# A gated linear attention and an MLP on one Trainium2 core: products of zeros at the start, another first product, stores in halves, another written-out order

## Chip, cores and metric

One core of one Trainium2 chip. The metric is the device time in microseconds (us) of one execution of the whole program, lower is better. "TensorE" does the matmuls, "VectorE", "ScalarE" and "GpSimd" the elementwise work, "SyncE" issues nearly all DMAs. In the profile they are PE (with PEld for the loading of weights), DVE, ACT, POOL and SP.

## The reference

A recurrence with a gate for each channel, over 4 batches, 8 heads, 768 positions, 48 channels a head; then, on its output seen as 768 rows of 384, a layer norm, a two-layer MLP with ReLU and a residual.

```python
for t in range(S):                                    # attention; state is 48 x 48 for each batch and head
    state = alpha[:, :, t, :, None] * state + np.einsum('bhd,bhe->bhde', k[:, :, t], v[:, :, t])
    y[:, :, t] = np.einsum('bhd,bhde->bhe', q[:, :, t], state)
x = y.transpose(0, 2, 1, 3).reshape(B, S, H * D)      # (4, 768, 384)
mu, var = mean(x), mean((x - mu) ** 2)                # over the last axis
xn = (x - mu) / np.sqrt(var + 1e-06) * g_ln
out = x + np.maximum(xn @ w_ch1, 0.0) @ w_ch2         # w_ch1 384 x 1536, w_ch2 1536 x 384
```

q, k, v and alpha come in float32. The two weight matrices come in float64 and are rounded to float32 on the chip. All matmuls are in float32.

## The kernel before

**Tiling.** The 768 positions are cut into 6 chunks of 128; a chunk of one batch is one attention block, 24 in all. A block is written as a generator (`attention`, from L220 on) that issues one step at each call: logarithm of the gates (L225, tile `la`), their sums over positions with a triangular matmul (L228, `lps`), two exponentials (L232, L233), k and q multiplied by them (GpSimd L235, VectorE L237), transposes of q and k (L251, `tps`) with copies out of PSUM (L255, L257), scores (L264, `aps`), masked copy (L268, `at`), output (L281 with the state, L286 with the scores, `yps`), copy to `x` (L290), the change of the state (L297, `sps`; L302; L307), statistics and normalisation (L311 to L318, `xn`), transposes of the normalised x (L325, `xps`) and their copy (L327, `xT`).

**Weights.** Twelve pieces of 768 KB are loaded, three in flight (`load_weights`, L151), and rounded by VectorE and ScalarE (`round_weights`, L163 to L178; six pieces of the first matrix, then six of the second). The first chunk's MLP is done plainly: 12 hidden products of 512 columns (`hidden`, L337), then the second layer for each batch in thirds (`project`, L349).

**Chunks 1 to 5** use fewer products. The first layer is done in two halves r = 0 and 1 by 15 products each (`hidden_product`, L510), numbered 0 to 14, in the order of the tuple FIRST. Product n multiplies one combination of blocks of the first weights (`combine_first`, GpSimd L462) with one combination of blocks of xT (`combine_x`, VectorE L486). Product 11 uses a block of xT as it is. Each product's accumulator, one of three in PSUM under the tag "m", is taken off by VectorE or ScalarE, and some of the results are added together later by GpSimd (`add_late`, seven of them in a half: L529, L532, L535, L540, L545, L548, L549). So product 4 is followed by L531 and L532, product 14 by L534 and L535, product 11 by the ScalarE copy L539 and by L540, which adds it to a sum that product 14 began; product 2's accumulator is added by L542 to what L540 wrote, and product 12's by L553 to what L549 wrote. ReLUs (L562) follow on ScalarE. The second layer is done for two batches at a time by seven products of six accumulating matmuls (`product`, L404), in the order 1, 4, 2, 6, 7, 5, 3; the combinations of the hidden values are VectorE's L390. The rows of the second batch of a pair are stored after product 5, those of the first (`o0`) after product 3, each with one DMA of 128 rows of 384 (`send`, L566). The left half of `o0`'s columns has its last addition after product 2 (L417), the right half after product 3 (L430).

**Order.** Every engine runs its instructions in the order in which the program issues them, and waits at each for what it needs. The order is written out by hand in the string ORDER: each letter calls the next step of one generator. Small letters are the attention blocks: a to d are the four batches of chunk 0, e to h those of chunk 1, and so on to x. Capitals A to L are the weight pieces (rounding in three steps, then the issue of the load three pieces on). M is the MLP (each product is two steps: the matmuls, then what takes them off), S the combinations of weights on GpSimd, X those of xT, N those of the hidden values, R the ReLUs. SyncE, too, issues its DMAs in this order and waits at each until its tile is free or written; the loads of q, k, alpha and v of the first chunk and of the first three weight pieces are issued ahead of the string.

**PSUM.** Tag "a" has three buffers for the gates' sums, the transposes and the scores (which take two at once), tag "s" two, tag "m" three for the MLP. A tile takes a buffer whose last reader stands earlier in the order, and waits for it.

The loop that runs the order:

```python
    with tc.manual_schedule():
        for turn in ORDER:
            next(turns[turn], None)
```

Of the kernel before, what the change touches and what calls it, by code (L numbers as in the profile page):

```python
# [9 lines left out]
FP32 = mybir.dt.float32  # L10
# [11 lines left out]


ORDER = (
    "ababdaacbaabccaabacdacbaabadcbbbdcdAabbbdaBcCccdabAeddbcbdcffcdfeegacfcbagdhfbde"
    "adbceBeegAdhfBCfdeabdfefcAheiBeafdeagjgbecfebcfcgeegfdefdgcghhihfdcgdegCCigMhMgD"
    "DhMjEMEjFMhiDkhfMgfighFheMFFfMMIMEIhIDMgEjhMGhMgjMhgfMGiHMMGGkMMMMHeiJMkMlHJMigM"
    "IMLJilHljMejKKjiLKeLjMhhfjSigSMhMlSMglSlhgiffMKkMhMhSSSMSSSMXiXkikXSXiimjMXXXSSM"
    "MXkMMSkjMMXkMkMMSMMjMmMMjXkmMSlmiMSMMiMkMMXkMjMMMlMlmRMmMMMokSjlMlMnlMnMljnkMMMR"
    "MjnMMMMSMMmMnMMmnRMMRRMoRSkiMlpklniMkpnjmMMRMmMRpkMRMNMMNmMlMiRkmMMiNMMnloMpRMSM"  # L30
    "njNMMkplMoRMMMkMMNmjNMMlMMNNmonnMljomqMMlqMMlnXMMXMXmXnXXMXqMMMXmmXMMooMMMMpMpMn"
    "MMXMMoMoMMMrMoXMnRqoRmoMpMMrpMMMMMMpMMpRnproMMmMMmqMMMrMMMqqMsMMnMnMpJqrRnqsMorM"
    "tMMMMmqMooRppMpotsRMMtRMtMrMRqMRNMoMNMRNMMrMpRMoNsMqMspqpMoMtMMRMMMNMNMMNMMMoMpn"
    "MpNsrrnMtrpqvrquXrXXrXMquXqXsMXsrMXrMqMMXMXuMMMMrMrMLMsMtXMMstMMMtqMsstMMMMMqvRR"
    "MMvMsuMsMtuMMRMMMrMMuwMMMMRMMMvwMvqMttqMMMruRMMRMMsMMRMMMMRMssRtwtsvutxvMRNsvMNN"
    "tMvNsRtRMMMvMtMMuusMMtMMwuuMrMMwwxNxMxvrtNNMMMNMMMtxsMMMuXMXXXMvMvuuXxXXMXvXuMMM"
    "MwwXwMMxMMxMXMMMMMMuvMMxMMuMMwRxMMMwwRMvMwMMMRxuxwxwwMuxMRxvMwMMMxxMMMMMRMMvMMuM"
    "RMMMvMMMxMMRuMRMMRMMNMMMNRMMNMMvMMNMMMwwMMvwMxxRNwRMMNMNNMMMMwxMMvxMXXXXXXMMMMXX"
    "XMMMMMMMMMXMMMMMMMMXMMMMMRRMMMMMMMMMMMMMRMMRMMMMMMMMMMRRMMMRMMRMMMMMMRMNMMMNRNMM"
    "MMNMMMMMMMRMNRMNMMNMMMMNMMMMMMMM"  # L40
)


# [1 line left out]
def kernel(  # L45
# [36 lines left out]
    nc = tc.nc  # L82
# [4 lines left out]
    P = 128  # L87
# [8 lines left out]
    cpool = ctx.enter_context(tc.tile_pool(name="const", bufs=1))  # L96
# [5 lines left out]
    ps = ctx.enter_context(tc.tile_pool(name="ps", bufs=2, space=bass.MemoryType.PSUM))  # L102
# [93 lines left out]
    nc.vector.memset(eps, EPS)  # L196
    least = cpool.tile([P, 1], FP32, name="least")
    nc.vector.memset(least, -8.0 * (896 << 20))


    eqs = [cpool.tile([P, NP, 2, 64], FP32, name=f"eq{b}") for b in range(B)]
# [157 lines left out]
    HJ, HM = NJ // 2, DM // 2  # L359
# [13 lines left out]
    def quarters(c, b):  # L373
        if (c, b) not in win:
            hT = hT_of[c]
            a11, a12, a21, a22 = (hT[:, js, i] for i in (b, b + 1)
                                  for js in (slice(0, HJ), slice(HJ, NJ)))
            win[c, b] = {1: a11, 2: a12, 4: a22}, a21
        return win[c, b]
# [14 lines left out]
    def product(c, b, n):  # L394

        if n == 1:
            for i in (0, 1):
                win["o", i] = work.tile([P, 2, HM], FP32, name="ob", tag="ob", bufs=3)
            u = [work.tile([P, 512], FP32, name="u", tag=f"u{i}", bufs=1) for i in range(2)]
            for i in range(4):  # L400
                win["u", i] = u[i // 2][:, i % 2 * HM:][:, :HM]
        acc = ps.tile([P, HM], FP32, name="ops", tag="m", bufs=3)
        for j in range(HJ):
            nc.tensor.matmul(acc, quarters(c, b)[0][n][:, j], win["b"][n][:, j],  # L404
                             start=(j == 0), stop=(j == HJ - 1))
        yield
        x0, x1 = (x_of[c, i].rearrange("p (s m) -> p s m", s=2) for i in (b, b + 1))
        o0, o1 = win["o", 0], win["o", 1]
        p1, u2, u3, u4 = (win["u", i] for i in range(4))
        add, add_late = nc.vector.tensor_add, nc.gpsimd.tensor_add  # L410
        if n == 1:
            nc.scalar.copy(out=p1, in_=acc)
            add_late(o0[:, 0], p1, x0[:, 0])
        elif n == 4:
            add(o1[:, 0], acc, x1[:, 0])
        elif n == 2:
            add(o0[:, 0], acc, o0[:, 0])  # L417
        elif n == 6:
            add(u2, acc, p1)
        elif n == 7:  # L420
            add(u3, acc, u2)
            add_late(o1[:, 1], u3, x1[:, 1])  # L422
            add_late(o1[:, 0], u3, o1[:, 0])
        elif n == 5:
            add(u4, acc, u2)
            add(o1[:, 1], acc, o1[:, 1])
            add_late(u4, u4, x0[:, 1])
            send(c, b + 1, o1)
        else:
            add(o0[:, 1], acc, u4)  # L430
            send(c, b, o0)
            del x_of[c, b], x_of[c, b + 1]
        yield

# [54 lines left out]
            yield  # L489

    RELUS = ((1, 0), (2, 0), (0, 0), (0, 1), (1, 1), (2, 1))
    FIRST = (3, 7, 5, 10, 9, 1, 4, 14, 11, 6, 13, 2, 8, 0, 12)

    def hidden_product(c, r, n):

        if n == FIRST[0] and r == 0:
            hT_of[c] = work.tile([P, NJ, B, P], FP32, name="hT", tag="hT", bufs=1)
        if n == FIRST[0]:
            for i in range(3):
                first_of["u", i] = work.tile([P, 512], FP32, name="u", tag=f"u{i}", bufs=1  # L500
                                             ).rearrange("p (j t) -> p j t", j=2)
        hT = hT_of[c].rearrange("p j b t -> p j (b t)")
        cs = [hT[:, t * NT + 2 * r:][:, :2, h * HB * P:(h + 1) * HB * P]
              for t in range(3) for h in range(2)]
        acc = ps.tile([P, 2, HB * P], FP32, name="hps", tag="m", bufs=3)
        a, b = first_of["a"][n], first_of["b", c][n]
        for i in range(2):
            j = 2 * r + i
            w = a[0][:, j * P:(j + 1) * P] if j < 3 else a[1]
            nc.tensor.matmul(acc[:, i], w, b, start=True, stop=True)  # L510
        yield
        u0, u1, u2 = (first_of["u", i] for i in range(3))
        c0, c1, c2, c3, c4, c5 = cs
        add, sub = nc.vector.tensor_add, nc.vector.tensor_sub
        add_late, sub_late = nc.gpsimd.tensor_add, nc.gpsimd.tensor_sub

        if n == 3:
            nc.scalar.copy(out=c5, in_=acc)
        elif n == 7:
            add(c4, acc, c5)  # L520
        elif n == 5:
            add(c2, acc, c4)
        elif n == 1:
            add(u0, acc, c2)
        elif n == 10:
            nc.scalar.copy(out=u1, in_=acc)
        elif n == 9:
            sub(u2, u1, acc)  # L528
            add_late(c4, c4, u2)  # L529
        elif n == 4:  # L530
            sub(c2, c2, acc)  # L531
            add_late(c2, c2, u1)  # L532
        elif n == 14:
            add(u2, acc, u2)  # L534
            add_late(c0, u0, u2)  # L535
        elif n == 6:
            add(c4, acc, c4)
        elif n == 11:
            nc.scalar.copy(out=c1, in_=acc)  # L539
            add_late(c0, c0, c1)  # L540
        elif n == 2:
            add(c0, acc, c0)  # L542
        elif n == 13:
            sub(c3, u0, acc)
            add_late(c1, c1, c3)  # L545
        elif n == 8:
            sub(u2, u2, acc)
            add_late(c1, c1, u2)  # L548
            add_late(c5, c5, u2)  # L549
        elif n == 0:  # L550
            sub(c3, c3, acc)
        else:
            sub(c5, c5, acc)  # L553
        yield
# [7 lines left out]
                    nc.scalar.activation(out=x, in_=x, func=AFT.Relu)  # L562
                    yield

    def send(c, b, ob):
        nc.sync.dma_start(out[b, c * P:(c + 1) * P], ob.rearrange("p s m -> p (s m)"))  # L566

    def mlp():
        for c in range(NCB):
            if c == 0:  # L570
                for j in range(NJ):
                    yield from hidden(c, j)
                thirds = [range(i * NJ // 3, (i + 1) * NJ // 3) for i in range(3)]
                for b0 in range(0, B, 2):
                    for js in thirds:
                        for b in range(b0, min(b0 + 2, B)):
                            yield from project(c, b, js)
                continue
            for r in range(NT // 2):
                for n in FIRST:  # L580
                    yield from hidden_product(c, r, n)
            for b in range(0, B, 2):
                for n in (1, 4, 2, 6, 7, 5, 3):
                    yield from product(c, b, n)
# [48 lines left out]
```

## Time and profile before

| | us |
|---|---|
| Timed runs, median (lowest to highest), 3 runs | 475.58 (474.87 to 476.09) |
| Profiled run, time | 473.87 |
| Profiled run, first to last instruction (the span) | 471.8 |
| TensorE's first matmul | 4.25 |
| First hidden product of chunk 0 (L337) | 46.34 |
| First product of the last chunk (L510) | 413.85 |
| First L404 product of the last chunk | 441.02 |
| Last addition (L430) starts | 468.60 |

The profile's lines name an engine, a line of the kernel, what is written and what is read with partitions and elements, a count and durations. In the order of time each row is: start in us, length in us, engine, line, operation, and in brackets how long the engine stood idle before it and what it waited for. The table by stage gives for each stretch its length and the busy us of PE, PEld, VectorE, ScalarE and GpSimd with the number of instructions, then the granted TensorE clock, the share of the DMA engines, and GB/s. A row of the waits reads: who waited for whom, us in total, times, longest.

### The profile page before, as it was taken

What the parts mean: (1) busy time and instruction counts of PE and PEld (TensorE: products, weight loads), DVE (VectorE), ACT (ScalarE), POOL (GpSimd) and SP (SyncE); (2) the same over time, 40 slices, a digit from 0 to 9 for tenths busy, and PEclk for the clock granted to TensorE, in tenths of its full rate; (3) what the DMA queues carried; (4) which work ended last, traced back from release to release, by engine and by line L of the source; (5) the groups of instructions that cost most, each with busy time, mean ns of one, the idle gap of its engine ahead of it and who ended that gap; (6) DMA issues with size and microseconds to landing.
All of it is one profiled execution on the core that took longest, in us unless ns stands there. A gap on an engine that the chain in (4) does not pass through costs nothing.

```text
span 471.8 us, 9234 instructions
## 1 busy us (share of the span) xinstructions
PE 459.0 (97%) x3712; PEld 388.5 (82%) x3712; DVE 327.1 (69%) x571; ACT 152.0 (32%) x325; POOL 203.8 (43%) x203
## 2 busy tenths in 40 slices
PE   5989999999999999999999999999999999999997
PEld 3758654566788899988899998899998899987996
DVE  4899997768456985567768378685656576675742
ACT  5676533421132631114341133351203331123300
POOL 5034010049779873127553116573214281145611
PEclk9999999999999999999999999999999999999999
DMA  8988365203112102030211320120010000000000
GB/s 267 334 234 265 78 192 173 83 23 113 52 36 67 35 18 84 8 114 18 86 35 35 100 71 17 35 85 1 33 36 1 1 1 17 18 33 2 0 35 33
DMA packets 32498, 33.84 MB, mean 72 GB/s; under 512 B 13108, under 2 KB 28596, under 8 KB 32456
## 3 DMA queue, kind: packets, MB, share of 16 engines
q1 hardware_dynamic: 31912, 33.12, 22.8%
q8 instruction: 29, 0.48, 0.4%
q10 hardware_dynamic: 544, 0.13, 0.1%
q14 instruction: 13, 0.11, 0.1%
HBM read 28.49 MB, written 4.76 MB: 70 GB/s over the span
## 4 chain that ended last, share of the span: by engine, by line
PE 90%; DMA 4%; DVE 2%; POOL 2%; ACT 2%; SPq 0%; issue 0%; POOLq 0%; DVEq 0%
PE ops L404 29%; PE hps L510 26%; PE hps L337 7%; PE ops L349 7%; PE aps L264 5%; PE yps L286 4%; PE yps L281 4%; PE tps L251 3%; PE lps L228 2%; PE sps L297 2%; PE xps L325 2%; DMA rk<-in_k_dram 2%; DMA ws<-in_moe_w_ch_dram 1%; DMA ra<-in_alpha_dram 1%; DVE w L163 1%; ACT ws L169 0%
## 5 line engine op out<-in xcount | busy, mean ns | idle before, releaser
L307 POOL TENSOR_TENSOR st<-st,gate 128x384 f32<-128x384 f32 x20 | 20.6, 1034 | 76.7 <-issue 30.6
L510 PE MATMUL hps<-sum,w 128*128 128x256 f32 x200 | 51.7, 381 | 0.0
L404 PE MATMUL ops<-w,hT 128*128 128x192 f32 x240 | 42.5, 327 | 0.0
L404 PE MATMUL ops<-w,sum 128*128 128x192 f32 x240 | 42.4, 326 | 0.0
L404 PE MATMUL ops<-ws,hT 128*128 128x192 f32 x240 | 42.3, 326 | 0.0
L562 ACT ACTIVATE hT<-hT 128x512 f32<-128x512 f32 x60 | 36.6, 632 | 16.5 <-POOL hT L548 6.6
L510 PEld LDWEIGHTS hps<-sum,w 128*128 128x128 f32 x200 | 37.1, 190 | 5.2
L404 PEld LDWEIGHTS ops<-w,hT 128*128 128x128 f32 x240 | 39.3, 190 | 0.7
L404 PEld LDWEIGHTS ops<-w,sum 128*128 128x128 f32 x240 | 39.3, 190 | 0.3
L404 PEld LDWEIGHTS ops<-ws,hT 128*128 128x128 f32 x240 | 39.3, 190 | 0.0
L268 DVE COPY_PREDICATED at<-consts,aps 128x512 f32<-128x512 int32 x48 | 32.2, 724 | 10.2 <-PE aps L264 9.9
L286 PE MATMUL yps<-rv,at 128*64 128x48 f32 x768 | 36.4, 219 | 0.0
L422 POOL TENSOR_TENSOR ob<-u,x 128x192 f32<-128x192 f32 x10 | 6.9, 686 | 67.6 <-issue 42.8
L235 POOL TENSOR_TENSOR qk<-rk,ek 128x384 f32<-128x384 f32 x24 | 26.7, 1113 | 19.5 <-ACT ek L232 19.5
L286 PEld LDWEIGHTS yps<-rv,at 128*64 128x64 f32 x768 | 33.0, 137 | 1.3 <-issue 0.7
L529 POOL TENSOR_TENSOR hT<-hT,u 128x512 f32<-128x512 f32 x10 | 12.8, 1284 | 48.6 <-DVE u L528 48.5
L337 PE MATMUL hps<-xT,w 128*128 128x512 f32 x72 | 32.6, 598 | 0.0
L349 PE MATMUL ops<-w,hT 128*128 128x384 f32 x96 | 32.3, 488 | 0.0
L510 PE MATMUL hps<-xT,w 128*128 128x256 f32 x120 | 31.2, 383 | 0.0
L251 PE MATMUL tps<-consts,qk 128*112 128x128 f32 x192 | 29.2, 281 | 1.5 <-DVE at L268 1.0
L264 PE MATMUL aps<-qkT 48*128 48x128 f32 x384 | 28.6, 285 | 1.5 <-DVE at L268 0.8
L251 PEld LDWEIGHTS tps<-consts,qk 128*112 128x112 f32 x192 | 22.8, 137 | 8.8 <-issue 4.1
(127 smaller groups left out, 956.2 us busy)
## 6 DMA issues: line engine op xcount, KB each, us to landing
ws<-in_moe_w_ch_dram SPq DMA_DIRECT2D x12, 768.0 KB
ra<-in_alpha_dram SPq DMA_DIRECT2D x24, 192.0 KB
rk<-in_k_dram SPq DMA_DIRECT2D x24, 192.0 KB
rq<-in_q_dram SPq DMA_DIRECT2D x24, 192.0 KB
rv<-in_v_dram SPq DMA_DIRECT2D x24, 192.0 KB
out_dram<-ob SPq DMA_DIRECT2D x24, 192.0 KB
row<-eq SPq DMA_DIRECT2D x20, 2.0 KB
gate<-row SPq DMA_DIRECT2D x20, 2.0 KB
```

Of the source, the lines that this page charges most:

```text
L235: nc.gpsimd.tensor_mul(qk[:, 1, :, :D], raws.pop(("k", c, b)), ek)
L251: nc.tensor.transpose(tps[:, p], qks[b][:, i, p].rearrange("p a b -> p (a b)")[:, :R], ident)
L264: nc.tensor.matmul(aps[i][:, p], qkT[rows, 1, p], qkT[rows, 0, p], start=True, stop=True)
L268: nc.vector.copy_predicated(out=at[:, i], data=aps[i], mask=mask.unsqueeze(1).broadcast_to([P, NP, P]))
L281: nc.tensor.matmul(yps[s, p].rearrange("p a b -> p (a b)"), qkT[:, 0, p, s], sts[b][:R, p].rearrange("p a b -> p (a b)"), start=True, stop ...
L286: nc.tensor.matmul(yps[s, p, i], at[:, i, p, s], vt[:, 2 * p + i], start=(c == 0), stop=(c == 0 or i == 1))
L307: nc.gpsimd.tensor_mul(st, st, gate.unsqueeze(2).broadcast_to([P, NP, 2 * D]))
L337: nc.tensor.matmul(hps, w1[:, f, j * P:(j + 1) * P], xT_of[c][:, f], start=(f == 0), stop=(f == NF - 1))
L349: nc.tensor.matmul(ops_of[b], hT_of[c][:, j, b], w2[:, j], start=(j == 0), stop=(j == NJ - 1))
L404: nc.tensor.matmul(acc, quarters(c, b)[0][n][:, j], win["b"][n][:, j], start=(j == 0), stop=(j == HJ - 1))
L510: nc.tensor.matmul(acc[:, i], w, b, start=True, stop=True)
L562: nc.scalar.activation(out=x, in_=x, func=AFT.Relu)
```

## The change

Five edits. A tile of zeros is set by VectorE, and nine matmuls of it by itself are issued first of all on TensorE; their result, in a buffer of tag "a", is read by nobody. FIRST starts with product 11, the others keep their order, so in each half product 11 moves from the ninth place to the first. The late addition L540 moves, in the code, from product 11 to product 14, behind that product's own late addition; the order of the seven late additions on GpSimd stays. The rows of `o0` are stored in two halves of 192 columns, the left one after product 2, the right one after product 3. And ORDER is another string, of the same length and with each letter as often as before; only its first lines are shown.

```diff
 ORDER = (
-    "ababdaacbaabccaabacdacbaabadcbbbdcdAabbbdaBcCccdabAeddbcbdcffcdfeegacfcbagdhfbde"
-    "adbceBeegAdhfBCfdeabdfefcAheiBeafdeagjgbecfebcfcgeegfdefdgcghhihfdcgdegCCigMhMgD"
+    "baacabbaadbcdbabcacababadcbdbadabbadbAaacabdcacccbcdBddceecdeCafefhbdAfbdcfbchbf"
+    "BahffeefcbedeededggCcAgffBbeAgBdiadbeadgfecagfeedcegffheghgcfCidcgdgcgkihDCMihMh"
...
+    zero = cpool.tile([P, P], FP32, name="zero")
+    nc.vector.memset(zero, 0.0)
+    idle = ps.tile([P, 512], FP32, name="lps", tag="a", bufs=3)
+    for _ in range(9):
+        nc.tensor.matmul(idle[:, :P], zero, zero, start=True, stop=True)
...
             add(o0[:, 0], acc, o0[:, 0])
+            send(c, b, o0, (0,))
...
-            send(c, b, o0)
+            send(c, b, o0, (1,))
...
-    FIRST = (3, 7, 5, 10, 9, 1, 4, 14, 11, 6, 13, 2, 8, 0, 12)
+    FIRST = (11, 3, 7, 5, 10, 9, 1, 4, 14, 6, 13, 2, 8, 0, 12)
...
             add_late(c0, u0, u2)
+            add_late(c0, c0, c1)
...
             nc.scalar.copy(out=c1, in_=acc)
-            add_late(c0, c0, c1)
...
-    def send(c, b, ob):
-        nc.sync.dma_start(out[b, c * P:(c + 1) * P], ob.rearrange("p s m -> p (s m)"))
+    def send(c, b, ob, halves=(0, 1)):
+        cols = slice(halves[0] * HM, (halves[-1] + 1) * HM)
+        nc.sync.dma_start(out[b, c * P:(c + 1) * P, cols],
+                          ob.rearrange("p s m -> p (s m)")[:, cols])
```

More of the change, by code (lines that the diff above doesn't have):

```diff
@@ L24 @@
 ORDER = (
-    "ababdaacbaabccaabacdacbaabadcbbbdcdAabbbdaBcCccdabAeddbcbdcffcdfeegacfcbagdhfbde"
-    "adbceBeegAdhfBCfdeabdfefcAheiBeafdeagjgbecfebcfcgeegfdefdgcghhihfdcgdegCCigMhMgD"
[L27 to L40, printed above, removed]
+    "baacabbaadbcdbabcacababadcbdbadabbadbAaacabdcacccbcdBddceecdeCafefhbdAfbdcfbchbf"
+    "BahffeefcbedeededggCcAgffBbeAgBdiadbeadgfecagfeedcegffheghgcfCidcgdgcgkihDCMihMh"
+    "MhEDlMMFMghFDfegfhFMlFiehIMElMiEMIiMMMjIMDGMEHgiMjjGhMgMheGHjGMiMgHMJfhMIMJjLHJK"
@@ new lines @@
+    "LijKhMKLhhMSggMfllegSMkSjMjhMMkSefSSSMMjgMlhhhMigMfXfMMjXiXXiSMSkXXXSMSMjSiikMSl"
+    "MSSnXjMjijMMXklkMkMmjKMSMMllkSMSMXMMXMMMMRMmmMMnMMkMMMSkmkniMkMRiMmljiRkjmknkomM"
+    "kMkMRMMRMMMnSMMMMnlMMRMlMMMMMMMMRjoopoMMMpRMimmlllmmRMMNpMnNkMMjNMRSMMnMkinnlNRM"
+    "pMMlMMMMilRMjpMMkmmjNlonnMjNpnNmMNMmlMkMolMMqMXMXmXXXnMXMMmpXnpmoMMMXMMMXMMMoXMM"
+    "mpMMoroMMMMrqMpqMMMMnXMoorrMMonrMooMpMRMRMRmMMmpqRrMMMtMMnnMpMMMRmMMMMMMMJqqMrMM"
+    "MMMppRoRrnRMMMstMMRptpopNRqMRMNpMrqsMMsMNsMMpnnqNMMMtMqMMRMsNrNMMsMqooMqMMNMMMpt"
@@ new lines @@
+    "tNMqoMvpMorMqorXrXrMtXMXXvXusXXrMsMMMMXMMXMqXMqMrMMMtMMvMMMsMMMutMMRtMMMMMMqsMMu"
+    "vMMMsrsMMsuRMtqsRtrttvMvMMMqvuvsqMMRMMvrMvMuMMMMutuMqRMMRRMuMMqRMuRMMMsNwttxutrM"
+    "RxMuMNNRMMNwMsMrMMxMMMsMMxstRNNrvMMswtsMwNMxtNMMMuvMsMtXMvvXvuXwXXvXMxMMXwMMwwXM"
+    "MMXMXMXMxMMMMuMMMMwMwMxMvRMuxMMRMMMRwuxMMMRwMRMMxMMMRMwMMMMMMMMMMMMuMRMxxwxuMxMv"
+    "MRLMMxMMuMMRNMNwMwMMMRvwRxuMNNxMMwMxvMMMMMRwwuMMvMMMwNNMNMMxwMxNMxMMvXXXXMXXMMXX"
+    "MMXMXMMMMXMMMMMMMMMMMMMMMMMMMMMMRRMMMMMMMMRMMMMMMMMRRMMRRMMMMMMMRMMMRMMMNMMNMMNM"
@@ L41 @@
+    "RMMMMMMMNMMNRMRMMNNMMMMNMMMMMMMM"
 )
```

## The prediction

> **What bounds the kernel now.** I read the page's shares first, then the busy time by stage, then the chain of waits, and the order of time at the places where TensorE is not busy. Times are microseconds from the start of the profiled execution, whose span is 471.8; the timed runs have a median of 475.58, so every step below is worked out on the span and carried over by the ratio.
>
> ```profile
> PE 459.0 (97%) x3712; PEld 388.5 (82%) x3712; DVE 327.1 (69%) x571; ACT 152.0 (32%) x325; POOL 203.8 (43%) x203
> ```
> TensorE is busy for all but 12.8 us. The table by stage (span of the stretch, then busy us of each engine) says where these are:
>
> ```profile
> 0.00:12.00 12.00, 6.97 (x16) 3.88 (x16) 5.10 (x13) 6.75 (x13) 6.80 (x14) 1.00 0.84 268
> 12.00:35.00 23.00, 20.13 (x305) 15.58 (x304) 20.83 (x37) 15.35 (x34) 4.94 (x5) 1.00 0.90 283
> 35.00:50.00 15.00, 14.42 (x195) 11.31 (x195) 14.66 (x29) 8.08 (x20) 6.01 (x6) 1.00 0.86 258
> 50.00:85.00 35.00, 35.00 (x235) 18.75 (x234) 30.78 (x51) 16.44 (x29) 3.16 (x3) 1.00 0.41 131
> ...
> 413.00:445.00 32.00, 31.00 (x152) 27.54 (x151) 20.90 (x32) 10.62 (x19) 19.29 (x16) 1.00 0.04 13
> 445.00:472.00 27.00, 23.49 (x145) 23.19 (x143) 10.65 (x21) 0.38 (x2) 4.05 (x7) 1.00 0.08 30
> ```
> Idle: 5.0 + 2.9 + 0.6 before 50, nothing until 413, 1.0 in the last chunk, 3.3 after the last matmul. In 35 to 50 VectorE is nearly full too (14.66 of 15). So the kernel is two stretches in a row: a start in which VectorE, from the arrival of the first weights on, has no pause, and from the first hidden product (46.34) on TensorE alone. The work of the second stretch is the same in both kernels: 468.5 - 46.3 - 1.2 = 421.0 us. That it is all real work follows from the merged chain: 12 hidden products and 12 projection pieces of 2.58 each, 150 products L510 of 0.863, 70 products L404 of 1.95 and some 94 of attention give 422. A new order alone gains nothing there.
>
> The start, on VectorE in order of time:
>
> ```profile
> 15.42 0.95 DVE L163 TENSOR_SCALAR w<-ws 128x768 int32<-128x768 int32 x1 [0.35 <-DMA ws<-in_moe_w_ch_dram]
> ...
> 17.88 1.34 DVE L268 COPY_PREDICATED at<-consts,aps 128x512 f32<-128x512 int32 x2
> 19.11 0.94 DVE L163 TENSOR_SCALAR w<-ws 128x768 int32<-128x768 int32 x1
> ```
> It waits for the first weights until 15.42 and then runs without a gap to beyond 60. The last thing the first hidden product needs of it, the fourth normalised x (L318), ends at 43.36.
>
> The last chunk, on GpSimd:
>
> ```profile
> 420.93 1.27 POOL L532 TENSOR_TENSOR hT<-hT,u 128x512 f32<-128x512 f32 x1 [0.44 <-DVE hT L531]
> 422.16 1.45 POOL L535 TENSOR_TENSOR hT<-u 128x512 f32<-128x512 f32 x1
> 423.69 1.27 POOL L540 TENSOR_TENSOR hT<-hT 128x512 f32<-128x512 f32 x1
> 425.04 1.27 POOL L545 TENSOR_TENSOR hT<-hT 128x512 f32<-128x512 f32 x1
> 426.42 1.27 POOL L548 TENSOR_TENSOR hT<-hT,u 128x512 f32<-128x512 f32 x1
> 427.64 1.28 POOL L549 TENSOR_TENSOR hT<-hT,u 128x512 f32<-128x512 f32 x1
> ```
> Six late additions follow each other, started by product 4 (L531). L553, which frees the accumulator of product 12, waits for the last, and TensorE waits for L553, the only such wait after the start:
>
> ```profile
> PEld hps L510 <- DVE hT L553: 1.4, 1, 1.4
> ```
>
> [...] two L228 matmuls take 0.65 in the chain at 44.35, while the first four take 2.93 with a wait of about 0.35 in it; the eight transposes at 9.39 take 1.91, later four take 0.44. Full rate begins near 11. [...] here 2.84 us lie between the last addition (468.96) and the end.
>
> **Products of zeros.** Nine of 128 columns, two instructions each as in the transposes. At the half rate of 1.91 / 8, less the drain of the last, about 0.21 each: 18 x 0.21 = 3.8 us. They need one memset (0.17 us as L205, at 0.9, VectorE idle until 7.5: no cost) and run from about 1.2 to 5.0. TensorE idles until 4.25 before. In the new order batch b's gates go first on ScalarE; they landed at 4.56 (its L225 waited until then), so the first L228, of batch a, is ready near 5.5: the zeros cost nothing. [...] worth up to 3.2 us of TensorE time (1.3 + 0.65 on three of the four first L228 pairs, 0.85 and more on the transposes). But TensorE does not end the start.
>
> **The start in the new order.** Up to the first hidden product both strings hold the same TensorE steps. VectorE's list up to the last x it needs, each at its trace duration: before, from the first rounding step, 28.3 us by list, 27.9 measured; after, 27.5, so 27.2 by the same ratio: the second batch's mask copies (1.34) go ahead of the rounding, one more q product (0.54) and a changed order come in. But when can the rounding start? After the copies of a and b: the gate product d goes before the transposes of a, the exponentials of d before the scores of a. By the durations (first exponentials 6.5, q of b 9.5, transposes of a from 9.3, exponentials of d to 12.4, scores a 12.5 to 13.7, copies to 15.0, scores b, which need an accumulator that these copies free, to 15.6, copies to 16.9) the rounding starts at 16.9 with full rate early, 17.4 without; not below 15.42 in any case, since the weights land then. So the last x is ready at 16.9 + 27.2 = 44.1; a transpose of x (0.55), scores (1.15) and 0.1 follow: the first hidden product at 45.9 instead of 46.34, **0.4 gained**. Bounds: 43.2 (rounding at 15.42 and without the slow cases of L237, 1.1 us) to 47.5.
>
> On SyncE the loads for batch b of the next chunk move ahead of two row copies; they stand behind the first three weight loads (issued until 11.2) in both strings and land for use at 19.8 and later, so they move no weights and cost 0. On GpSimd the k products keep their places but for d's, which comes earlier.
>
> **Product 11 first.** Nothing is added, and ScalarE's copy of it has slack. Before the change TensorE never waited for the sums of x at the start of a chunk, so the freedom is worth 0. But product 4, which starts the six additions, now comes one product (0.863) later, while product 12 keeps its place. In chunks 1 to 4 attention work lies between (2.7 us or more by the new string in the first half, counted at chain durations), so 0 there, with up to 0.4 at chunk 3. In the last chunk none is left: the wait at the half grows by **0.86**. At its end product 12 needs the accumulator of product 2, freed by L542, which waits for the third addition; before, 439.73 against a weight load at 439.95, a slack of 0.2: **0.65 lost**.
>
> **Halves.** Ten more sends, 0.34 us each on SyncE; behind the early half wait loads and the sends of the other row block; SyncE stood 194 us before L426 without TensorE waiting, so 0. The last send has 98 KB less; at the 381 GB/s moved between 18 and 20 **0.26 gained** (bounds 0 and 0.5). [...]
>
> **Sum**: 471.8 - 0.4 + 0.86 + 0.65 - 0.26 = 472.65, and 475.58 x 472.65 / 471.8 = **476.4**.
>
> **Rivals.** Below 0.3%, about 1.4 us, a measurement of this kernel can't tell a change from none. (1) Forecast, 476.4: chance 0.40. (2) Faster: VectorE starts rounding at 15.42 and loses nothing to GpSimd; first hidden product at 43.2, -3.1 + 1.5 - 0.3 = -1.9, so 473.7. For it: 3.2 us of half-rate work go. Against: VectorE is full from 15.42 on in the old kernel already. It decides below 43.7: 0.20. (3) Slower: the copies of batch b, now ahead of the first rounding, wait on the chain through the gate product and exponentials of d, and VectorE idles until 18.3; all behind it moves: the first hidden product at 47.3, +1.0 + 1.5 - 0.3 = +2.2, so 477.8, and more if the last weight pieces (L174 ends at 99.88, the projection that needs them starts at 100.49) then hold TensorE. It decides from 46.5 on: 0.33. (4) The late additions are met by slack that I don't see, and only start and tail count: -0.7, 474.9: 0.07.
>
> So faster 0.20, within 0.3% 0.47 (cases 1 and 4), slower 0.33. Range 473.4 to 479.0, from case 2 to a bad case 3; forecast's own range 475.0 to 477.6.
>
> **What would show it.** Right: the first L337 at 45 to 46.5; a single L553 wait of about 2.3 us on the weight loads at the half of the last chunk, a new one of some 0.65 for L542; the end 2.6 after the last addition. Wrong: the first L337 below 44; no longer wait for L553; any TensorE wait between the first L337 and the last chunk.

## The result, and the profile after

The changed kernel takes 482.17 us in the median of four runs (481.50 to 484.48), the kernel before, on the same chip, 475.24 (474.87 to 476.09): ratio 1.0152, 95% interval 1.0114 to 1.0190. The forecast was 476.4 with a range to 479.0; the change costs about 6.9 us where 0.8 were forecast.

The profiled execution has a span of 480.8 us against 471.8. That is 9.0 and not 6.9 because the profiled execution of before took 473.87 us, 1.4 less than its median, and that of after, 482.57, was near its own. I split the span at four places:

| stretch, us | before | forecast | after |
|---|---|---|---|
| start to the first hidden product | 46.34 | 45.9 | 51.58 |
| from there to the first product of the last chunk | 367.51 | 367.5 | 370.05 |
| from there to the last chunk's first L404 product (now L411) | 27.17 | 28.68 | 28.72 |
| from there to the end | 30.78 | 30.52 | 30.41 |

So the two lower rows came as forecast, and the two upper rows grew by 5.2 and 2.5 us, where a gain of 0.4 and no change were forecast. Of the 5.2 us some 2, by an estimate from 9.0 and 6.9, belong to the two executions that were profiled: the start moves from one to the next with the landing of the first weights. The page's shares and its row of the granted clock (one digit for each fortieth of the span), after:

```profile
PE 465.9 (97%) x3730; PEld 393.4 (82%) x3730; DVE 326.7 (68%) x572; ACT 151.0 (31%) x325; POOL 198.5 (41%) x203
...
PEclk9898999999999999999999999999999999999999
```

TensorE's share is the same 97%: the share hides the loss. The table by stage shows where it is (length of the stretch, then PE, PEld, VectorE, ScalarE, GpSimd, granted clock, share of the DMA engines, GB/s):

```profile
12.00:35.00 23.00, 18.98 (x286) 15.13 (x287) 20.05 (x34) 12.84 (x30) 5.01 (x5) 0.93 0.86 274
35.00:50.00 15.00, 12.76 (x182) 11.04 (x177) 13.62 (x28) 7.27 (x17) 3.72 (x4) 0.89 0.75 229
50.00:85.00 35.00, 35.00 (x240) 19.41 (x238) 31.19 (x49) 17.62 (x32) 3.58 (x4) 1.00 0.42 128
...
16.00:18.00 2.00, 2.00 (x37) 1.90 (x38) 2.00 (x3) 0.00 (x0) 0.00 (x0) 0.50 1.05 410
44.00:46.00 2.00, 2.00 (x41) 2.00 (x39) 1.37 (x4) 0.35 (x1) 0.00 (x0) 0.50 1.06 303
```

In 35 to 50 VectorE falls from 14.66 to 13.62 and TensorE from 14.42 to 12.76: VectorE, which was to run without a pause, has pauses. And the granted clock is 0.50 in two stretches (from 15.4 to 18.8 and from 42.7 to 46.1); in the profile of before it was 1.00 in every stage from 12 us on. VectorE in order of time, after:

```profile
17.09 0.93 DVE L163 TENSOR_SCALAR w<-ws 128x768 int32<-128x768 int32 x1
...
23.27 1.34 DVE L275 COPY_PREDICATED at<-consts,aps 128x512 f32<-128x512 int32 x2 [0.45 <-PE aps L271]
...
28.82 0.72 DVE L309 TENSOR_TENSOR st<-sps,st 64x192 f32<-64x192 f32 x2 [0.51 <-PE sps L304]
...
36.73 2.02 DVE L178 SCALAR_TENSOR_TENSOR w<-w,g,ws 128x256 f32<-128x256 f32 x3
...
39.54 1.09 DVE L325 TENSOR_SCALAR xn<-x,mv,rstd 128x384 f32<-128x384 f32 x1
...
46.49 0.72 DVE L309 TENSOR_TENSOR st<-sps,st 64x192 f32<-64x192 f32 x2 [1.08 <-PE sps L304]
...
47.72 0.47 DVE L325 TENSOR_SCALAR xn<-x,mv,rstd 128x384 f32<-128x384 f32 x1
```

The brackets are the waits: 0.45, 0.51 and 1.08, all for TensorE, in sum 2.04. Three entries are also longer than their like: the L178 triple (2.02, elsewhere 1.28), a normalised x (1.09, the last takes 0.47) and a q product at 30.27 (0.89, elsewhere 0.54). The waits of TensorE's weight loads after the start, after:

```profile
PEld hps L518 <- DVE hT L530: 1.8, 1, 1.8
PEld hps L518 <- DVE hT L561: 1.5, 1, 1.5
PEld hps L518 <- DVE hT L550: 1.4, 2, 0.7
...
PEld xps L332 <- DVE xn L325: 0.6, 1, 0.6
```

Before there was one, for L553 (now L561). The two for L550 (the old L542) lie in the last chunk, one in each half; the forecast had the one at its end, and a longer wait for L553 in place of the other. The first and the fourth lie in the middle, where the forecast had none. From the first hidden product to chunk 1's first product, and then by chunks, the middle's 2.5 us are -1.0, +2.9, -0.3, +0.8 and +0.1: the growth lies above all in chunk 1, where the 1.8 us are.

### The profile page after: what moved, and what is told of

The parts are those of the page before. It is cut to its first block, busy times and chain, and to the rows that moved or that the text cites. A ratio compares the mean times of both kernels' runs of the same rounds, so it can differ in the third digit from the quotient of the medians.

```text
span 480.8 us, 9286 instructions
## 1 busy us (share of the span) xinstructions
PE 465.9 (97%) x3730; PEld 393.4 (82%) x3730; DVE 326.7 (68%) x572; ACT 151.0 (31%) x325; POOL 198.5 (41%) x203
## 3 DMA queue, kind: packets, MB, share of 16 engines
q1 hardware_dynamic: 33352, 33.12, 22.6%
## 4 chain that ended last, share of the span: by engine, by line
PE 90%; DVE 3%; POOL 3%; ACT 1%; DMA 1%; issue 1%; SPq 0%; POOLq 0%; DVEq 0%
PE ops L411 29%; PE hps L518 25%; PE hps L344 7%; PE ops L356 7%; PE aps L271 5%; PE yps L293 4%; PE tps L258 4%; PE yps L288 4%; PE lps L235 3%; PE sps L304 2%; PE xps L332 2%; PE lps L205 1%; DMA rq<-in_q_dram 1%; POOL hT L540 1%; POOL hT L544 1%
## 5 line engine op out<-in xcount | busy, mean ns | idle before, releaser
L411 PE MATMUL ops<-ws,hT 128*128 128x192 f32 x240 | 42.7, 328 | 0.0
L411 PE MATMUL ops<-w,sum 128*128 128x192 f32 x240 | 42.5, 327 | 0.0
L411 PE MATMUL ops<-w,hT 128*128 128x192 f32 x240 | 42.3, 326 | 0.0
L411 PEld LDWEIGHTS ops<-ws,hT 128*128 128x128 f32 x240 | 39.4, 190 | 0.9
L411 PEld LDWEIGHTS ops<-w,hT 128*128 128x128 f32 x240 | 39.4, 190 | 0.2
L411 PEld LDWEIGHTS ops<-w,sum 128*128 128x128 f32 x240 | 39.3, 190 | 0.1
L293 PE MATMUL yps<-rv,at 128*64 128x48 f32 x768 | 38.1, 226 | 0.0
L293 PEld LDWEIGHTS yps<-rv,at 128*64 128x64 f32 x768 | 34.7, 145 | 0.4 <-issue 0.2
L314 POOL TENSOR_TENSOR st<-st,gate 128x384 f32<-128x384 f32 x20 | 17.9, 901 | 33.6 <-DVE st L309 20.6
L271 PEld LDWEIGHTS aps<-qkT 48*128 48x128 f32 x384 | 24.4, 188 | 7.9 <-issue 4.2
L288 PE MATMUL yps<-st,qkT 112*64 112x96 f32 x320 | 30.4, 262 | 0.0
```

The lines of the kernel that those rows point to most:

```text
L271: nc.tensor.matmul(aps[i][:, p], qkT[rows, 1, p], qkT[rows, 0, p], start=True, stop=True)
L288: nc.tensor.matmul(yps[s, p].rearrange("p a b -> p (a b)"), qkT[:, 0, p, s], sts[b][:R, p].rearrange("p a b -> p (a b)"), start=True, stop ...
L293: nc.tensor.matmul(yps[s, p, i], at[:, i, p, s], vt[:, 2 * p + i], start=(c == 0), stop=(c == 0 or i == 1))
L314: nc.gpsimd.tensor_mul(st, st, gate.unsqueeze(2).broadcast_to([P, NP, 2 * D]))
```

## The experiments

Times stand against the runs of the kernel before on the same chip (medians 474.57 to 474.74). "Start" is the time to the first hidden product, "middle" the next stretch of the table, "last" the one behind it, each from one profiled execution. The middle is 367.51 or 367.52 us in all seven kernels with the old order there and the old FIRST. The start moves: in the five kernels with the old first steps and no zeros it is 46.34, 46.43, 46.93, 47.97 and 48.51, since the first rounding waits for its weights until 15.42 to 17.60. A difference of 1 or 2 us in that column says little without the times. Counted from the first rounding it is 30.90 to 30.93 in four of these five; the fifth, with 14 ahead of 4, takes 31.94 and has a stretch at a clock of 0.50 from 27.4 to 30.8.

**The zeros: alone, and taken out of the changed kernel.**

```diff
 before
+    for _ in range(9):
+        nc.tensor.matmul(idle[:, :P], zero, zero, start=True, stop=True)
 after
-    for _ in range(9):
-        nc.tensor.matmul(idle[:, :P], zero, zero, start=True, stop=True)
```

> The kernel before with the nine products of zeros alone; sequence, FIRST and stores are the old ones. Two theories of the start, where the changed kernel loses 5.3 us up to its first hidden product. Order theory (the new sequence makes the start long, zeros do nothing): the first hidden product stays at 46.3 us, the granted clock stays 1.00 in every slice, time within 0.5 us of before. Clock theory [...]: a stretch of about 3.5 us at a clock of 0.50 shows in the first 50 us, the first hidden product is at 48 us or later, time 2 to 3 us over before.

> The changed kernel with its nine products of zeros taken out, all else left. Order theory: the first hidden product stays at about 51 us, the time at about 482 us. Clock theory: no slice of the start is granted less than full rate, the first hidden product comes at 47 to 48.5 us, the time falls by 2.5 to 4 us to 478 to 479.5 us. In both the first products of the start run at half rate until about 11 us, as in the kernel before.

Alone: 474.9 against 474.6, ratio 1.0007 (1.0000 to 1.0014); start 47.55, within what the landing of the weights does. Taken out: 482.35, ratio 1.0180 (1.0149 to 1.0211), the same as with them; start 51.02. So the zeros neither gain nor cost anything that counts, and the order theory holds on the time. But the clock is not settled by this: the kernel without zeros has a stretch at 0.50 too (16.7 to 20.1), and the old sequence with zeros has one from 19.2 to 22.6, as the clock theory said, yet without its loss. What it lacks is somebody who waits: VectorE has no pause there. Nor is the drop the new order's own: three of the eighteen runs of the kernel before that stand beside the filled kernel below were granted 0.993 to 0.996, the others 1.00.

**The start of the new sequence in front of the old rest.** The zeros and the first 155 steps are new, the rest is old, FIRST and stores too.

> The zeros and the first 155 steps of the new sequence (all that lies ahead of the first hidden product), and after them the old sequence's remaining steps; FIRST and stores old. If all that is lost up to the first hidden product comes from zeros and those 155 steps, it is again at 51 to 52 us, and the span is 5.3 us over before; the middle and the last chunk are as before. If the loss of the start is made up behind it by slack, the span grows by less than 4 us.

479.3, ratio 1.0106 (1.0079 to 1.0132): +4.7 us. Start 51.79, middle 367.52, last 27.17. The loss of the start comes from those 155 steps and is made up by nothing behind it; middle and last chunk are as before to 0.01.

**Which of the 155 steps.** First the new 50 with the old rest, then the old 50 with the new steps to 155, then the changed kernel with the old first 80.

> The kernel before with the first 50 steps of the new sequence and then the remaining steps of the old one; no zeros, old FIRST, whole stores. These 50 steps put the second half of batches a and b (two masked copies more) ahead of the first rounding. Theory A (they decide: the rounding starts 1.7 us later, at about 17.1 in place of 15.4, and VectorE carries that and more on to the last normalised x): first hidden product at 49 us or later, time 2.5 us or more over before. Theory B (steps 51 to 155 decide: VectorE stands idle for TensorE's products there, and its operations fall beside GpSimd's): first hidden product at no more than 48 us, time at most 1.7 us over before.

> The counterpart: the first 50 steps of the old sequence, then the remaining steps of the new one's first 155, then the old sequence; no zeros, old FIRST, whole stores. Theory A: rounding starts at 15.4 us as before, first hidden product at no more than 48 us, time at most 1.7 us over before. Theory B: rounding starts at 15.4 us and the first hidden product still comes at 49 us or later, time 2.5 us or more over before, with VectorE idle of 1.5 us or more between rounding and the last normalised x.

> The changed kernel whole (zeros, product 11 first, halves), but with the first 80 steps of the old sequence ahead of the new one's remaining steps. Theory A: the first hidden product comes at 48 us or earlier, the time falls from 482 to at most 479.5 us, and what lies behind the first hidden product takes as long as in the changed kernel. Theory B: first hidden product at 49.5 us or later, time at 480.5 us or more.

| | start | time, against before |
|---|---|---|
| new 50, old rest | 50.66 | 478.44, +3.7 |
| old 50, new to 155, old rest | 52.63 | 481.81, +7.1 |
| changed kernel, old first 80 | 49.49 | 481.24, +6.5 |

Theory A holds for the first, theory B for the second and third, so neither part decides: each spliced start is slow, and 3.7 and 7.1 don't add up to the 4.7 of both parts together. What they share is seen in the first of them. Its stages, and VectorE in order of time:

```profile
26.00:28.00 2.00, 2.00 (x19) 1.54 (x19) 1.97 (x4) 0.00 (x0) 0.00 (x0) 0.50 0.88 239
28.00:30.00 2.00, 2.00 (x12) 1.07 (x12) 0.39 (x2) 0.87 (x2) 0.33 (x1) 0.50 0.06 23
```

```profile
31.04 1.35 DVE L268 COPY_PREDICATED at<-consts,aps 128x512 f32<-128x512 int32 x2 [2.64 <-PE aps L264]
```

At a clock of 0.50 TensorE delivers the scores so late that VectorE stands 2.64 us. The second shows the same at 46.82 (1.86 for TensorE's state sums, at 0.50), and the third at 25.32 (1.21 for the scores, after 6.8 us at 0.50). In the kernel before VectorE never waits between 15.42 and the first hidden product.

**Holding the clock up, and taking GpSimd's work away.** Nineteen more products of zeros, put where TensorE stood idle in the start (`fill(n)` issues n of them; `fill(9)` takes the place of the first nine, and the result lies in a buffer of tag "m"); and with them, GpSimd's four multiplications by the gate in chunk 0 left out.

```diff
...
+        fill({(1, 0): 5}.get((c, b), 0))
         nc.tensor.matmul(lps[:, :DM], tri, la, start=True, stop=True)
...
+        fill({(0, 1): 3, (0, 2): 3}.get((c, b), 0))
         for p in range(NP):
...
+        fill({(0, 0): 8}.get((c, b), 0))
         for f in range(NF):
...
-            nc.gpsimd.tensor_mul(st, st, gate.unsqueeze(2).broadcast_to([P, NP, 2 * D]))
+            if c > 0:
+              nc.gpsimd.tensor_mul(st, st, gate.unsqueeze(2).broadcast_to([P, NP, 2 * D]))
```

> The changed kernel with 19 more products of zeros, put into TensorE's queue at four of the places where it stood idle in the start (3 each ahead of the scores of batches b and c of chunk 0, 5 ahead of the running sums of chunk 1's batch a, 8 ahead of the transposes of chunk 0's batch a), so that TensorE isn't thinly used there. Clock theory: the stretches at a granted clock of 0.50 in the start go, and the first hidden product comes at 48.5 to 50 us in place of 51.6, the time falls by 1.5 to 3 us. Order theory (the waits and slowed operations are the sequence's own): the clock stretches may go, but the first hidden product stays within 0.8 us of 51.3 and the time within 0.8 us of 482.

> As the kernel with 19 more products of zeros, and GpSimd's four multiplications of the state by the gate in chunk 0 are left out (so the states of the later chunks are not decayed by chunk 0's gate). Theory that VectorE's operations of the start are slowed beside GpSimd's: the normalisation that took 1.09 us and the q product that took 0.89 take 0.47 and 0.54, the first hidden product comes 0.8 to 1.2 us earlier than with them. Rival (this slack is taken up by waits for TensorE): the first hidden product comes at the same time within 0.4 us.

With the filling the granted clock is 1.00 in all four runs (0.989 to 0.996 in the changed kernel's), and the stages show it:

```profile
16.00:18.00 2.00, 2.00 (x61) 1.88 (x58) 1.19 (x2) 0.17 (x1) 0.00 (x0) 1.00 1.05 409
44.00:46.00 2.00, 2.00 (x53) 1.77 (x50) 1.96 (x6) 0.69 (x2) 0.00 (x0) 1.00 1.03 329
```

VectorE's waits between the first rounding and the last normalised x are down from 2.04 to about 0.1. The time is 481.19, ratio 1.0136 (1.0123 to 1.0150), 1.0 below the changed kernel; by times alone the two intervals overlap. The four runs of the changed kernel lie the same way: 481.50 and 481.78 us at a granted clock of 0.996, 482.57 at 0.993, 484.48 at 0.989. So the clock is one part of the loss, by an estimate from these times about 1 us of 7, and both theories were half right. What the nineteen products themselves take in TensorE's queue is not separated here. What is left in VectorE's list is this:

```profile
27.04 1.26 DVE L167 TENSOR_SCALAR ws<-ws 128x768 int32<-128x768 int32 x1
...
37.04 2.03 DVE L178 SCALAR_TENSOR_TENSOR w<-w,g,ws 128x256 f32<-128x256 f32 x3
...
39.85 1.09 DVE L331 TENSOR_SCALAR xn<-x,mv,rstd 128x384 f32<-128x384 f32 x1
```

and on GpSimd of the same execution:

```profile
26.27 1.60 POOL L247 TENSOR_TENSOR qk<-rk,ek 128x384 f32<-128x384 f32 x1 [1.79 <-ACT ek L244]
...
37.74 1.04 POOL L247 TENSOR_TENSOR qk<-rk,ek 128x384 f32<-128x384 f32 x1 [6.68 <-ACT ek L244]
39.90 1.72 POOL L320 TENSOR_TENSOR st<-st,gate 128x384 f32<-128x384 f32 x2 [1.12 <-DVE st L315]
```

Three of VectorE's entries lie beside a GpSimd product and take 0.70, 0.75 and 0.62 more than alone (0.56, 1.28, 0.47): 2.07 in sum. Without the gate products the normalised x takes 0.48. The other two lie beside k products, which no run takes away, and stay at 2.02 and 1.25. But the traces tell the neighbours apart: in the first 130 us of all sixteen profiles the same operations with no GpSimd operation beside them take 0.56 to 0.58 (L167, 182 cases), 0.47 to 0.50 (one of the L178 triple, 264), 0.45 to 0.48 (x, 59) and 0.52 to 0.56 (q, 55), and every slower one lies beside one. Masked copies take 0.70 to 0.75 either way (121 cases without, 187 beside). It is plainest at 157.89 in the changed kernel: a q product of 0.54 us alone takes 2.61 and ends 0.41 us after GpSimd's subtraction of 2.64 us beside it. Why the one is slower beside the other was not shown.

But the 0.6 us gained there hardly arrive: 481.03 against 481.19, and from the first rounding to the first hidden product 31.94 against 32.26. (The first hidden product itself comes 1.15 earlier, 49.18 against 50.33, which looks like the theory's 0.8 to 1.2; but 0.83 of it is a first rounding at 17.24 in place of 18.07.) The rival holds; TensorE's queue behind the last x takes 3.38 in place of 2.98.

**Product 11 first, in the old sequence, and with 14 ahead of 4.**

```diff
-    FIRST = (3, 7, 5, 10, 9, 1, 4, 14, 11, 6, 13, 2, 8, 0, 12)
+    FIRST = (11, 3, 7, 5, 10, 9, 1, 4, 14, 6, 13, 2, 8, 0, 12)
 second kernel
+    FIRST = (11, 3, 7, 5, 10, 9, 1, 14, 4, 6, 13, 2, 8, 0, 12)
```

> The kernel before with product 11 first in FIRST and its late addition moved behind product 14; old sequence, no zeros, whole stores. Theory of the prediction: nothing in the start and in chunks 1 to 4, the stretch from the last chunk's first hidden product to the first product of its last group grows by 1.5 us (27.2 to 28.7), the span by 1.5 us. Rival: the old sequence was fitted to the old FIRST, so the wait of the last chunk grows by more, or waits of 0.5 us and more appear in chunks 1 to 4: span up by 2.5 us or more. Other rival: the 1.5 us of the changed kernel came from its sequence, and here the last chunk is as before.

> The kernel before with product 11 first and its late addition behind product 14, and products 4 and 14 exchanged in FIRST. Theory: product 11 stood between product 14 and product 2 and gave GpSimd's two additions to c0 one product's time; without it product 2's addition on VectorE comes late and the products behind it wait for its bank. With 14 one place earlier this wait goes: the weight loads' waits for that addition (2.2 us in three in the kernel with product 11 first alone) fall under 0.5 us, and the span falls by 1.5 to 2.5 us against that kernel. Rival (GpSimd's additions are late because GpSimd is full there): the waits stay above 1.5 us in sum or move to the additions of product 12, the span falls by less than 0.8 us.

First kernel: 477.01, ratio 1.0053 (1.0036 to 1.0070). Middle 369.27 (+1.76), last 28.50 (+1.33). Its waits:

```profile
PEld hps L510 <- DVE hT L542: 2.2, 3, 0.8
...
PEld hps L510 <- DVE hT L553: 1.5, 1, 1.5
```

The wait for L542 comes three times, once at the end of chunk 4 and twice in the last chunk. Chunks 1 to 4, from one chunk's first product to the next one's, grow by 0.36, 0.14, 0.67 and 0.60: the price is paid in the middle as well, which the prediction had at 0, and the first rival (waits in chunks 1 to 4) is right there. With 14 ahead of 4 the wait for L542 is gone, but L553 rises to 1.8, with 0.7 behind L551 and 0.5 behind GpSimd's L535; 478.1, ratio 1.0066 (1.0052 to 1.0081), no faster. The rival holds: another order of the products moves the wait to the additions of product 12.

**The changed kernel with product 11 back, and with the q product out of the way.** In the first, old FIRST and late addition, and four sums of x one step earlier, which product 5 needs; in the second, one letter two places later.

> The changed kernel with product 11 back at its old place (old FIRST, its late addition behind it); in four chunks one sum of x goes ahead of one step of the products, since product 5 comes one place earlier; zeros, halves and the rest of the new sequence stay. Theory: the cost of product 11 first is the same in the new sequence as in the old one (about 1.8 us in chunks 1 to 4 and 1.3 in the last), so the stretch from the first hidden product to the last chunk's is about 368.3 us (370.05 in the changed kernel, 367.51 in the kernel before), the last chunk's up to its first group about 27.2, the time 479 to 479.7 us. Rival: the growth of the middle is the new sequence's own, that stretch stays at 369.5 us or more and only the last chunk falls, time 480.5 us or more.

> The changed kernel with one step of the sequence moved two places later: the q product of chunk 3's batch b (the one that took 2.61 us beside GpSimd's subtraction of 1152 columns) behind product 5's addition in chunk 1's second half. Theory: the wait of 1.8 us for that addition goes and counts in full: first product of chunk 1 to its first group 42.7 us in place of 44.46, time 480.3 to 480.8 us. Rival: the 2.61 us put off the next addition on VectorE in the same way, a wait of 1 us or more stands behind another addition, time within 0.7 us of 482.

In the first both theories fell. With product 11 back the time is 494.1, ratio 1.0404 (1.0371 to 1.0437); middle 380.71, last 27.23:

```profile
PEld hps L518 <- DVE xT L494: 4.8, 3, 1.6
PEld hps L518 <- DVE ws L494: 3.2, 3, 1.2
```

L494 writes the sums of x. The new sequence makes them late, and product 11, which needs none, covers that. So the cost of product 11 first is not a fixed term: in the old sequence it costs 3.1 us of span, in the new one taking it out costs 10.7 in the middle and gives back 1.5 at the end. With the q product later the wait of 1.8 is gone and a wait of 1.3 for u (L536) stands in its place; chunk 1 up to its first group is 43.87 in place of 44.46. The time is 483.09, ratio 1.0203 (1.0150 to 1.0257), not to be told from the changed kernel's: the rival, though 0.4 above its bounds, with 0.6 us gained in the middle and a start of 52.73. Of the middle's 2.5 us some 1.6 are seen as idle time of TensorE (at the waits for L530 and L325); the rest I could not assign, and the 1.8 of product 11 in the old sequence is not a part of it that can be subtracted.

**Halves alone.**

> The kernel before with rows sent in two halves of columns, nothing else. Theory of the prediction: the stretch from the start of the last addition to the end falls from 3.20 to about 2.9 us, all else as before, time 0.3 us lower (ratio 0.9994). Rival: the half takes as long as the whole row and the time is the same within 0.05 us; other rival: the eight added stores on SP's queue put off a load of the later chunks and the time rises.

474.27 against 474.74, ratio 0.9993 (0.9984 to 1.0002): inside what can be told from no change. In the profile the last addition starts at 468.67 of a span of 471.5, so 2.83 to the end in place of 3.20, with middle and last at 367.51 and 27.16. The saving is there and is the forecast's size. (Ten stores are added, not the eight of the expectation; the middle shows no load that they put off.)

**A version faster than both.** In the kernel before GpSimd's six late additions hold up the half of the last chunk. Halves, and one of the six on VectorE, in the last chunk only:

```diff
         elif n == 8:
             sub(u2, u2, acc)
             add_late(c1, c1, u2)
-            add_late(c5, c5, u2)
+            (add if c == NCB - 1 else add_late)(c5, c5, u2)
```

> The kernel before with rows sent in halves, and in the last chunk alone product 8's addition to c5 on VectorE in place of GpSimd. In the kernel before GpSimd is busy without a gap from product 14's addition to the end of that half, and VectorE idles 1.92 us there for this addition; TensorE's weight loads then wait 1.4 us. Theory (GpSimd's queue sets that wait): it goes, the stretch from the last chunk's first hidden product to the first product of its last group falls from 27.17 to about 25.8 us, and the time by 1.7 us with the halves (ratio 0.9964). Rival: the added 0.7 us on VectorE puts off its other additions and the wait stays: ratio 0.9990 or more.

473.12 against 474.68, ratio 0.9966 (0.9954 to 0.9978). In order of time, VectorE before, then with the change (L550 is the moved addition), and the only wait of the products' weight loads for VectorE that is left:

```profile
428.95 0.69 DVE L553 TENSOR_TENSOR hT<-hT,hps 128x512 f32<-128x512 f32 x1 [1.92 <-POOL hT L549]
```

```profile
427.77 0.68 DVE L548 TENSOR_TENSOR u<-u,hps 128x512 f32<-128x512 f32 x1
428.48 0.69 DVE L550 TENSOR_TENSOR hT<-hT,u 128x512 f32<-128x512 f32 x1
429.09 0.68 DVE L552 TENSOR_TENSOR hT<-hT,hps 128x512 f32<-128x512 f32 x1
429.69 0.68 DVE L554 TENSOR_TENSOR hT<-hT,hps 128x512 f32<-128x512 f32 x1
```

```profile
PEld hps L511 <- DVE hT L552: 0.2, 1, 0.2
```

The idle 1.92 us ahead of product 12's subtraction is gone, the last chunk's stretch falls from 27.17 to 26.00. GpSimd's queue did set that wait.

## Why the prediction was wrong, by its own steps

- **Products of zeros: cost nothing, gain nothing that ends the start.** Right: ratio 1.0007 alone, and the same time with and without them in the changed kernel. The eight transposes at 9.44 take 1.18 us, where eight at 9.39 took 1.91 before.
- **The start in the new order: 0.4 gained.** This step failed: 5.2 lost in the profile, some 3 to 4 by the times (6.9 less 2.5 and 1.5 behind it, plus 0.4 at the end). Its terms, from three profiles:

| us | before | forecast | after | after, clock held |
|---|---|---|---|---|
| first rounding starts | 15.42 | 16.9 | 17.09 | 18.07 |
| from there to the end of the last normalised x | 27.94 | 27.2 | 31.10 | 29.28 |
| from there to the first hidden product | 2.98 | 1.8 | 3.39 | 2.98 |

The first term came near in this profile; over the eight kernels with the new first 50 steps it is 17.09 to 18.25, so it was some 0.8 too small (it also moves between executions of the old order, with the landing of the first weights: 15.42, 16.00 and 17.60 in three of the kernels). The second took the list's durations from the old order with no wait. In the new order 2.07 us are added by entries that lie beside GpSimd's (seen in the column on the right; the old order has 0.49 of the kind, a q product of 1.03 at 38.22, so 1.6 more), and in the changed kernel's own profile 2.04 by waits for TensorE, which go where the clock is held. The third left out what else stands in TensorE's queue behind the last x. TensorE in order of time there, before and after:

```profile
43.75 0.60 PE L251 MATMUL tps<-consts,qk 128*112 128x128 f32 x4
44.18 0.81 PE L228 MATMUL lps<-la,consts 128*128 128x384 f32 x2
```

```profile
48.61 0.65 PE L258 MATMUL tps<-consts,qk 128*112 128x128 f32 x4
49.09 0.81 PE L235 MATMUL lps<-la,consts 128*128 128x384 f32 x2
```

These run ahead of the last transposes of x in both kernels. The 2.98 us could be read in the profile of before; with them in place of 1.8 the forecast's own terms give 47.1 and a loss of 0.7 in place of the gain of 0.4. The sentence "TensorE does not end the start" was the error here and in the waits: TensorE ended VectorE's waits, and its own queue stands behind the last x.
- **Rival (3)** named the slower side, and a part of it is seen: VectorE was to idle until 18.3, and the rounding began at 17.09 here, at 18.02 to 18.25 in three kernels with the same first 50 steps. What it did not have is the loss behind the first rounding (34.49 to the first hidden product in place of 30.92), and the range to 479.0 was too short for that.
- **"A new order alone gains nothing there"** (behind the first hidden product) was right, but it can lose, and the term stood at 0: middle +2.5. This is the second step that failed. The forecast's 0 for product 11 in chunks 1 to 4 failed as well, 1.76 in the old sequence. The argument that attention work lies between did not hold.
- **Product 11 in the last chunk: +1.51.** Right in size: +1.55. The two terms were 0.86 at the half, which came as a new wait of 0.72 for L550 and an almost unchanged one for L561 (1.49, before 1.41) and not as one longer wait, and 0.65 at the end for product 2's accumulator, where 0.72 came.
- **"Worth 0" for product 11's freedom.** Right for the old sequence, which had no wait for the sums; wrong for the new one, where taking it away adds 9.2 us behind the first hidden product. (Its reason looked at waits in the old order alone.)
- **Halves: -0.26.** Right in the profile: -0.36 after (2.84 in place of 3.20), -0.37 alone; by the times no change can be told.
- The sum by times: the kernel with the clock held is +6.5, of which middle 2.56, last 1.56, tail -0.38 leave 2.8 for the start (1.34 from the first rounding on, 32.26 against 30.92, and the rest, about 1.5, for the later rounding); the clock adds about 1.0. What stays open: some 0.9 us of the middle, and how much of the 1.34 is the neighbours' doing.
- Small slips of the working, without weight for the sum: 27.5 by the ratio of 27.9 to 28.3 is 27.1; the idle time of the last chunk is 1.0, not the 1.2 taken off in the 421.0; VectorE stands idle for 0.43 us ahead of 59.18.

## What to carry to other kernels

A list of durations taken from one order is not the length of another: price the neighbours too (does the entry now lie beside an operation of the other engine that slows it, and by how much in this trace), and treat each engine that is not the bound as one that can release the bound late. An order written out by hand is fitted as a whole: each spliced start was slower than before, and product 11 at the head of FIRST cost 3 us in one sequence and saved 9 in the other. The cheap gain was at the one wait that the profile of before names: look at what its releaser was waiting for, and move one operation off that queue.

## What the runs showed that I had not expected

The clock falls back to half in the middle of the start with TensorE far from idle. The longest pause ahead of the stretch at 42.7 is 1.74 us, in an interval (36 to 42) in which TensorE is busy for 4.26 of 6, and the stretches last some 3.4 us, or 7 in the kernel with the new first 50 steps. The table by stage of the changed kernel just ahead of it:

```profile
40.00:42.00 2.00, 1.32 (x15) 1.16 (x17) 1.97 (x4) 0.00 (x0) 2.00 (x3) 1.00 0.80 268
42.00:44.00 2.00, 2.00 (x36) 1.88 (x34) 1.97 (x5) 0.86 (x3) 0.27 (x1) 0.68 1.09 353
```

Other pauses of the same size drew none: without the zeros TensorE is busy for 0.32 of the 2 us from 40 to 42, with the nineteen products for 0.69 of the 2 us from 30 to 32, and in both the clock stays at 1.00 there and in the 2 us behind. In the changed kernel the granted clock falls at 15.41 and at 42.72 and is back at 1.00 at 18.82 and at 46.13. The 3.41 us ahead of the second fall, and the stretch itself:

```profile
39.31:42.72 3.41, 2.04 (x23) 1.76 (x25) 3.31 (x7) 0.03 (x1) 2.69 (x3) 1.00 0.89 290
42.72:46.13 3.41, 3.41 (x63) 3.41 (x60) 2.65 (x6) 1.31 (x5) 0.00 (x0) 0.50 1.07 308
```

Ahead of the first fall TensorE is busy for 2.37 us in the same length (12.00 to 15.41). From 22.23 to 25.65 it is busy for 2.32, and the clock stays at 1.00 behind that. So the busy time alone doesn't tell where the clock falls (and the ends of matmuls are modelled in the profile); what sets it was not shown. Nineteen small products of zeros in the pauses were enough to keep the clock at 1.00 in four runs of four.
